# Reordering and cutting the last K and V loads of a streaming low-rank attention decode kernel

## The chip, the cores and the metric

The kernel runs on one core of a Trainium2 chip. The metric is device time in microseconds (us) of one execution, as the median of several. The profiles are single executions taken by the hardware profiler. Their span leaves out about 2 us that the device time includes (for the profiled execution of the kernel before: 258.22 us with a span of 256.2). All readings of "when" are in us from the start of the span. Program lines appear as L278 and so on. They differ between kernels, because lines were added. In the views PE is TensorE, PEld its weight loads, DVE VectorE, ACT ScalarE and SPq SyncE. The granted clock is the share of TensorE's full clock that the chip allowed (0.947 on average in the profile of the kernel before).

## The reference, cut to what matters

```python
B, H, Sq, Skv, Dh, R = 1, 32, 1, 4096, 192, 64
kp = einsum("rn,bhnd->bhrd", e_proj, k)      # project 4096 keys to 64 rows
vp = einsum("rn,bhnd->bhrd", f_proj, v)
scores = einsum("bhqd,bhrd->bhqr", q, kp) * Dh ** -0.5
p = softmax(scores)                          # over the 64 rows
o = einsum("bhqr,bhrd->bhqd", p, vp)         # one query per head
```

All tensors are bf16. K and V are 50 MB each and are read once. Everything else is small.

## The kernel before

The 32 heads are worked as 16 pairs, `m` = 0 to 15. `EP` and `FP` are `e_proj` and `f_proj` in on-chip memory, transposed; they are loaded first, as `EF`. The token index is split as 128 partitions times `J` = 32 rows, so one load brings a whole head: 128 partitions with 12,288 contiguous bytes each, 1.5 MB. Three buffers for K and three for V (`NPB`) let the loads run far ahead (35.9 us from issue to landing in the median of the K loads). In the cut below some waits for buffers are left out.

```python
# SyncE issues all loads, K pair then V pair
for m in range(NPAIR):
    slot = m % NPB
    if m >= NPB: sp.wait_ge(sem_kp, m - NPB + 1)          # buffer free again
    for i in range(2):
        sp.dma_start(K_sb[slot][:, i, :, :], seq_src(k, 2*m+i)).then_inc(sem_k[slot], 16)
    if m >= NPB: sp.wait_ge(sem_vp, vdone(m - NPB))
    for i in range(2):
        semv = sem_v[slot] if m < LASTP else sem_vlast[i]   # last pair: one semaphore a head
        sp.dma_start(V_sb[slot][:, i, :, :], seq_src(v, 2*m+i)).then_inc(semv, 16)
    if m == 0:
        sp.dma_start(Qbc[:], q2.partition_broadcast(R)).then_inc(sem_q, 16)
...
# TensorE: both heads of a pair in one matmul (384 columns), summed over 32 rows
for m in range(NPAIR):
    pe.wait_ge(sem_k[slot], 32 * (m // NPB + 1))
    for j in range(J):
        pe.matmul(kp_ps[pss][:, :, :], EP[:, j, :], K_sb[slot][:, :, j, :], start=(j == 0), stop=(j == J-1))
    if m < LASTP:
        pe.wait_ge(sem_v[slot], 32 * (m // NPB + 1))
        for j in range(J):
            pe.matmul(vp_ps[pss][:, :, :], FP[:, j, :], V_sb[slot][:, :, j, :], start=(j == 0), stop=(j == J-1))
    else:                                                  # last pair: head by head
        for i in range(2):
            pe.wait_ge(sem_vlast[i], 16)
            for j in range(J):
                pe.matmul(bank[:, 0, :], FP[:, j, :], V_sb[slot][:, i, j, :], start=(j == 0), stop=(j == J-1))
    for go in trig_out.get(m, []):                         # once for each group of 8 heads
        pe_out_group(pe, go)                               # 8 matmuls p x vp into out_ps
```

After the K matmuls, VectorE forms the scores. Once for each group of 8 heads, VectorE and ScalarE compute the softmax (about 3 us in a chain: 248.08 to 250.90 for the last group in the profile). ScalarE copies each V projection to SBUF (`VP`), and at the very end the sum to `O_sb`, which SyncE stores.

## Time and profile before

| | before |
|---|---|
| time, first four runs | 258.09 us median (258.04 to 258.35) |
| span of the profile | 256.2 us |
| one pair of loads (two DMAs) | 7.38 us |
| 32 matmuls over two heads, clock 1.0 | 5.4 us |
| last landing (last completion write of the last load) | 249.6 us |
| from there to the end | 6.6 us |

The first lines are from the profile's page of the kernel before. The rows of digits cut the span into 40 slices: the digit is the busy tenth of the 16 DMA engines, and below it is what they moved. The last line is the chain of work that ended last, by engine.

```profile
span 256.2 us, 2558 instructions
...
DMA  7999999999999999999999999999999999999970
GB/s 162 385 426 319 402 428 424 424 424 421 428 428 428 430 423 422 422 426 425 426 426 428 430 423 420 426 426 428 425 424 428 428 425 422 424 426 425 428 296 4
...
DMA 81%; PE 16%; SPq 2%; issue 0%; ACT 0%
```

The DMA engines are full from the second slice on, until the loads end within the last but one. So the stream of loads is the bound, and TensorE waits for it, as the view of waits of the same kernel shows (waiter, what it waited for, total us, number of waits, longest):

```profile
PE kp_ps L278 <- DMA K_sb<-in_k_dram: 27.9, 14, 7.0
PE vp_ps L286 <- DMA V_sb<-in_v_dram: 27.0, 15, 2.1
```

What is left is the end. This is the timeline of the kernel before (start, duration, engine, line, operation, output and inputs, count, and in brackets the idle time before and what ended it):

```profile
241.98 5.39 PE L278 MATMUL kp_ps<-K_sb,EP 128*64 128x384 bf16 x32 [1.94 <-DMA K_sb<-in_k_dram]
...
247.21 5.44 PE L298 MATMUL vp_ps<-V_sb,FP 128*64 128x192 bf16 x64
...
250.33 0.57 DVE L217 CAST PTd<-PT_g 64x1 bf16<-64x1 f32 x8
252.69 0.32 ACT L186 ACTIVATE VP<-vp_ps 64x192 bf16<-64x192 f32 x1 [2.31 <-PE vp_ps L298]
...
253.16 0.82 PE L252 MATMUL TX<-VP,PTd 64*32 64x192 bf16 x8 [0.50 <-ACT VP L186]
254.01 0.32 ACT L188 ACTIVATE O_sb<-TX 32x192 bf16<-32x192 f32 x1 [1.00 <-PE TX L252]
254.35 0.36 SPq L156 DMA_DIRECT2D out_dram<-O_sb  x1
```

The last K pair lands at 241.94. TensorE works on it until 247.2, and only then on the last V pair, although the first of its heads has landed at 245.6 by the trace's landing records: 64 matmuls of one head each, until 252.66. Then comes a fixed train: copy, eight matmuls, copy, store.

### The profile page before, as it was taken

To read this page: it belongs to the slowest core of one execution; us is meant where nothing else is said; L and a number is where in the kernel's file an instruction comes from. 1 tells how busy PE (TensorE), PEld (TensorE's weight loads), DVE (VectorE), ACT (ScalarE), POOL (GpSimd) and SP (SyncE) were. 2 spreads that over 40 slices of the span, in tenths; PEclk is the share of its full clock that TensorE was granted. 3 is DMA by queue.
4 is the path that set the end of the run, shared out by engine and by line. 5 is a ranking of instruction groups with operands and counts; after the bars stand their busy time and mean duration, and the time that the engine had idled before them with its cause. 6 is when DMAs were issued, how large, how long until landed. Compare 5 with 4: busy or idle time off the path is not lost.

```text
span 256.2 us, 2558 instructions
## 1 busy us (share of the span) xinstructions
PE 190.4 (74%) x1120; PEld 122.5 (48%) x1120; DVE 21.9 (9%) x137; ACT 13.6 (5%) x35; POOL 1.9 (1%) x14
## 2 busy tenths in 40 slices
PE   0559449668879666887966678897766799697695
PEld 0535226445546444554644445564444455364485
DVE  0400000000010020000020011000020002000021
ACT  2400000000000010000000010000000001000001
POOL 2000000000000000000000000000000000000000
PEclk9979959999979999997999999799999979799999
DMA  7999999999999999999999999999999999999970
GB/s 162 385 426 319 402 428 424 424 424 421 428 428 428 430 423 422 422 426 425 426 426 428 430 423 420 426 426 428 425 424 428 428 425 422 424 426 425 428 296 4
DMA packets 9514, 102.67 MB, mean 401 GB/s; under 512 B 1120, under 2 KB 1120, under 8 KB 1120
## 3 DMA queue, kind: packets, MB, share of 16 engines
q1 hardware_dynamic: 9504, 102.51, 96.6%
q8 instruction: 9, 0.15, 0.2%
q14 instruction: 1, 0.01, 0.0%
HBM read 102.50 MB, written 0.01 MB: 400 GB/s over the span
## 4 chain that ended last, share of the span: by engine, by line
DMA 81%; PE 16%; SPq 2%; issue 0%; ACT 0%
DMA K_sb<-in_k_dram 81%; PE kp_ps L278 13%; PE vp_ps L298 2%; SPq L147 2%; PE TX L252 0%; SPq L141 0%; SPq L140 0%; ACT VP L186 0%; ACT O_sb L188 0%
## 5 line engine op out<-in xcount | busy, mean ns | idle before, releaser
L278 PE MATMUL kp_ps<-K_sb,EP 128*64 128x384 bf16 x512 | 89.5, 335 | 27.9 <-DMA K_sb<-in_k_dram 27.9
L286 PE MATMUL vp_ps<-V_sb,FP 128*64 128x384 bf16 x480 | 88.9, 348 | 27.0 <-DMA V_sb<-in_v_dram 27.0
L278 PEld LDWEIGHTS kp_ps<-K_sb,EP 128*64 128x64 bf16 x512 | 56.4, 113 | 60.2 <-DMA K_sb<-in_k_dram 29.2
L286 PEld LDWEIGHTS vp_ps<-V_sb,FP 128*64 128x64 bf16 x480 | 54.9, 117 | 60.9 <-issue 30.7
L236 DVE CUSTOM_DVE_ANT_0 scr<-kp_ps,Qbc 64x192 bf16<-64x192 f32 x32 | 10.0, 347 | 193.5 <-PE kp_ps L278 179.6
L177 ACT ACTIVATE VP<-vp_ps 64x384 bf16<-64x384 f32 x15 | 7.3, 484 | 219.7 <-PE vp_ps L286 219.7
L266 PE MATMUL TX<-ident,EF_sb 128*128 128x128 bf16 x32 | 3.8, 310 | 8.2 <-DMA EF_sb<-in_f_proj_dram 8.2
L266 PEld LDWEIGHTS TX<-ident,EF_sb 128*128 128x128 bf16 x32 | 3.3, 164 | 8.4 <-DMA EF_sb<-in_f_proj_dram 8.2
L298 PE MATMUL vp_ps<-V_sb,FP 128*64 128x192 bf16 x64 | 5.4, 246 | 0.0
L298 PEld LDWEIGHTS vp_ps<-V_sb,FP 128*64 128x64 bf16 x64 | 5.3, 110 | 0.1
L252 PE MATMUL TX<-VP,PTd 64*32 64x192 bf16 x32 | 3.3, 243 | 0.5 <-ACT VP L186 0.5
L252 PEld LDWEIGHTS TX<-VP,PTd 64*32 64x32 bf16 x32 | 2.4, 92 | 1.6 <-issue 1.6
L208 DVE RECIPROCAL rsum<-ssum 8x1 f32<-8x1 f32 x4 | 0.6, 151 | 25.1 <-ACT Pm_g L161 25.1
L236 DVE DVE_READ_ACCUMULATOR2_ANT S_g<- 64x1 f32 x32 | 2.4, 75 | 0.0
L217 DVE CAST PTd<-PT_g 64x1 bf16<-64x1 f32 x32 | 2.3, 139 | 0.1
L227 DVE CAST EP<-TX 128x256 bf16<-128x256 f32 x4 | 1.7, 425 | 6.9 <-PE TX L266 6.8
L171 ACT ACTIVATE EP<-TX 128x256 bf16<-128x256 f32 x4 | 1.5, 385 | 8.0 <-PE TX L266 7.9
L161 ACT ACTIVATE Pm_g<-ST_g,negmx 8x64 f32<-8x64 f32 x4 | 1.3, 336 | 8.4 <-DVE negmx L204 8.4
L228 DVE CAST FP<-TX 128x256 bf16<-128x256 f32 x4 | 1.7, 414 | 0.0
L213 DVE STREAM_TRANSPOSE PT_g<-Pm_g 32x32 f32<-32x32 f32 x8 | 1.6, 200 | 0.2
L200 DVE STREAM_TRANSPOSE ST_g<-S_g 32x32 f32<-32x32 f32 x8 | 1.6, 199 | 0.2
L172 ACT ACTIVATE FP<-TX 128x256 bf16<-128x256 f32 x4 | 1.5, 377 | 0.0
(16 smaller groups left out, 8.2 us busy)
## 6 DMA issues: line engine op xcount, KB each, us to landing
K_sb<-in_k_dram SPq DMA_DIRECT2D x32, 1536.0 KB, 35.9
V_sb<-in_v_dram SPq DMA_DIRECT2D x32, 1536.0 KB, 36.5
Qbc<-in_q_dram SPq DMA_DIRECT2D x1, 768.0 KB, 22.4
EF_sb<-in_e_proj_dram SPq DMA_DIRECT2D x1, 512.0 KB, 4.9
EF_sb<-in_f_proj_dram SPq DMA_DIRECT2D x1, 512.0 KB, 6.8
out_dram<-O_sb SPq DMA_DIRECT2D x1, 12.0 KB, 1.4
```

The source lines that it names most:

```text
L147: sp.dma_start(K_sb[slot][:, i, :, :], seq_src(k, 2 * m + i)).then_inc(sem_k[slot], 16)
L177: act.activation(VP_sb[:, 2 * m:2 * m + 2, :], vp_ps[pss][:, :, :], ACT.Copy).then_inc(sem_vps_free, 1)
L200: ins = dve.transpose(ST_g[g][:, rb * TB:(rb + 1) * TB], S_g[g][rb * TB:(rb + 1) * TB, :])
L217: ins = dve.tensor_copy(PTd[:, h, h:h + 1], PT_g[g][:, i:i + 1])
L227: dve.tensor_copy(EP[:, j0:j1, :], TX[r % 2][:, 0:HJ, 0:R])
L228: dve.tensor_copy(FP[:, j0:j1, :], TX[r % 2][:, 0:HJ, R:2 * R]).then_inc(sem_evD, 1)
L236: ins = dve.tensor_tensor_reduce(out=scr[2 * pss + i][:], in0=kp_ps[pss][:, i, :], in1=Qbc[:, h, :], scale=1.0, scalar=0.0, op0=ALU.mult, ...
L252: ins = pe.matmul(out_ps, PTd[:, h, :], VP_sb[:, h, :], start=(h == 0), stop=(h == H - 1))
L266: ins = pe.matmul(TX[r % 2][:, jj, :], EF_sb[:, j::J], ident[:], start=True, stop=True)
L278: ins = pe.matmul(kp_ps[pss][:, :, :], EP[:, j, :], K_sb[slot][:, :, j, :], start=(j == 0), stop=(j == J - 1))
L286: ins = pe.matmul(vp_ps[pss][:, :, :], FP[:, j, :], V_sb[slot][:, :, j, :], start=(j == 0), stop=(j == J - 1))
L298: ins = pe.matmul(bank[:, 0, :], FP[:, j, :], V_sb[slot][:, i, j, :], start=(j == 0), stop=(j == J - 1))
```

## The change

The intent is to have less work left when the last byte lands. The change

- moves the load of the last K pair (15) ahead of the load of V pair 14;
- cuts K 15 in two, V 14 in three and V 15 in five pieces of rows, each with its own semaphore, so that TensorE can follow the stream piece by piece;
- does V 15 with matmuls over both heads again (32 instead of 64);
- does six of the last eight out matmuls after the first piece of V 15.

```diff
+    CK = [16, 16]              # rows of the pieces of K 15
+    CA = [16, 8, 8]            # V 14
+    CB = [8, 8, 8, 4, 4]       # V 15
...
+            for m in range(NPAIR - 2, NPAIR):              # SyncE: K 14 whole, then K 15 in pieces
...
+                    for c, (j0, j1) in enumerate(cuts(CK)):
+                        for i in range(2):
+                            sp.dma_start(K_sb[slot][:, i, j0:j1, :],
+                                         seq_src(k, 2 * m + i)[:, j0:j1, :]).then_inc(sem_kb[c], 16)
+            for m, sems, cs in ((NPAIR - 2, sem_va, CA), (NPAIR - 1, sem_vb, CB)):
+                sp.wait_ge(sem_vp, vdone(m - NPB))
+                for c, (j0, j1) in enumerate(cuts(cs)):
+                    for i in range(2):
+                        sp.dma_start(V_sb[slot][:, i, j0:j1, :],
+                                     seq_src(v, 2 * m + i)[:, j0:j1, :]).then_inc(sems[c], 16)
...
+            def pe_vp(m, sems, cs):                        # TensorE
+                for c, (j0, j1) in enumerate(cuts(cs)):
+                    pe.wait_ge(sems[c], 32)
+                    for j in range(j0, j1):
                         ins = pe.matmul(vp_ps[pss][:, :, :], FP[:, j, :], V_sb[slot][:, :, j, :],
                                         start=(j == 0), stop=(j == J - 1))
+                    if m == mB and c == 0:
+                        pe.wait_ge(sem_epi_p, NG)
+                        pe.wait_ge(sem_vps_free, vdone(mA))
+                        pe_out_rows(G * (NG - 1), 2 * mB)  # heads 24 to 29
+                ins.then_inc(sem_vp, 1)
+            pe_kp(mA)
+            pe_kp(mB)
+            pe_vp(mA, sem_va, CA)
+            pe_vp(mB, sem_vb, CB)
+            pe.wait_ge(sem_vps_free, vdone(mB))
+            pe_out_rows(2 * mB, H, last=True).then_inc(sem_fin, 1)
```

The first three groups of out matmuls stay where they were (after pairs 5, 9 and 13). The bytes and the arithmetic are the same.

More of the change, by code (lines that the diff above doesn't have):

```diff
@@ L43, in bass_standalone__low_rank_proj_linformer__decode_kernel @@
     AX = mybir.AxisListType
+    CK = [16, 16]
+    CA = [16, 8, 8]
+    CB = [8, 8, 8, 4, 4]
+    cuts = lambda cs: [(sum(cs[:i]), sum(cs[:i + 1])) for i in range(len(cs))]
+    assert sum(CK) == J and sum(CA) == J and sum(CB) == J
     NPB = 3
@@ L92, in bass_standalone__low_rank_proj_linformer__decode_kernel @@
         sem_v = [sem(f"sem_v{i}") for i in range(NPB)]
-        sem_vlast = [sem(f"sem_vlast{i}") for i in range(2)]
+        sem_va = [sem(f"sem_va{c}") for c in range(len(CA))]
+        sem_kb = [sem(f"sem_kb{c}") for c in range(len(CK))]
+        sem_vb = [sem(f"sem_vb{c}") for c in range(len(CB))]
         sem_kp = sem("sem_kp")
@@ L112, in bass_standalone__low_rank_proj_linformer__decode_kernel @@
         LASTP = NPAIR - 1
-        vdone = lambda m: m + 1 if m < LASTP else NPAIR + 1
+        vdone = lambda m: m + 1
         def trigger_map(lag):
@@ L122, in bass_standalone__low_rank_proj_linformer__decode_kernel @@
         trig_b = trigger_map(LAG_B)
-        trig_out = trigger_map(LAG_P)
+        trig_out = {5: [0], 9: [1], 13: [2]}
         @block.gpsimd
@@ L141, in _ @@
             sp.dma_start(EF_sb[R:2 * R, :], f_proj).then_inc(sem_ef, 16)
-            for m in range(NPAIR):
+            for m in range(NPAIR - 2):
                 slot = m % NPB
@@ L150, in _ @@
                 for i in range(2):
-                    semv = sem_v[slot] if m < LASTP else sem_vlast[i]
-                    sp.dma_start(V_sb[slot][:, i, :, :], seq_src(v, 2 * m + i)).then_inc(semv, 16)
+                    sp.dma_start(V_sb[slot][:, i, :, :], seq_src(v, 2 * m + i)).then_inc(sem_v[slot], 16)
                 if m == 0:
                     sp.dma_start(Qbc[:], q2.partition_broadcast(R)).then_inc(sem_q, 16)
+            for m in range(NPAIR - 2, NPAIR):
+                slot = m % NPB
+                sp.wait_ge(sem_kp, m - NPB + 1)
+                if m == NPAIR - 2:
+                    for i in range(2):
+                        sp.dma_start(K_sb[slot][:, i, :, :], seq_src(k, 2 * m + i)).then_inc(sem_k[slot], 16)
+                else:
+                    for c, (j0, j1) in enumerate(cuts(CK)):
[3 more added lines that the diff above has]
+            for m, sems, cs in ((NPAIR - 2, sem_va, CA), (NPAIR - 1, sem_vb, CB)):
+                slot = m % NPB
+                sp.wait_ge(sem_vp, vdone(m - NPB))
+                for c, (j0, j1) in enumerate(cuts(cs)):
+                    for i in range(2):
+                        sp.dma_start(V_sb[slot][:, i, j0:j1, :],
+                                     seq_src(v, 2 * m + i)[:, j0:j1, :]).then_inc(sems[c], 16)
             sp.wait_ge(sem_osb, 1)
@@ L174, in _ @@
                 pss = m % NPS
-                if m < LASTP:
-                    act.wait_ge(sem_vp, m + 1)
-                    act.activation(VP_sb[:, 2 * m:2 * m + 2, :], vp_ps[pss][:, :, :], ACT.Copy).then_inc(sem_vps_free, 1)
+                if m == NPAIR - 2:
+                    act_exp(act, NG - 1)
+                act.wait_ge(sem_vp, m + 1)
+                act.activation(VP_sb[:, 2 * m:2 * m + 2, :], vp_ps[pss][:, :, :], ACT.Copy).then_inc(sem_vps_free, 1)
+                if m < NPAIR - 2:
                     for g in trig_b.get(m, []):
                         act_exp(act, g)
-                else:
-                    for g in trig_b.get(m, []):
-                        act_exp(act, g)
-                    for i in range(2):
-                        act.wait_ge(sem_vp, m + 1 + i)
-                        bank = vp_ps[(pss + i) % NPS]
-                        act.activation(VP_sb[:, 2 * m + i, :], bank[:, 0, :], ACT.Copy).then_inc(sem_vps_free, 1)
             act.wait_ge(sem_fin, 1)
@@ L247, in pe_out_group @@
         def pe_out_group(pe, g):
+            assert g < NG - 1
             pe.wait_ge(sem_epi_p, g + 1)
@@ L251, in pe_out_group @@
                 h = G * g + i
-                ins = pe.matmul(out_ps, PTd[:, h, :], VP_sb[:, h, :], start=(h == 0), stop=(h == H - 1))
-            if g == NG - 1:
-                ins.then_inc(sem_fin, 1)
+                pe.matmul(out_ps, PTd[:, h, :], VP_sb[:, h, :], start=(h == 0), stop=False)
         @block.tensor
@@ L267, in _, with pe_kp @@
                 ins.then_inc(sem_tr, 1)
-            for m in range(NPAIR):
+            def pe_kp(m):
                 slot = m % NPB
                 pss = m % NPS
-                if m == 0:
-                    pe.wait_ge(sem_evD, NR)
-                    pe.wait_ge(sem_evA, NR)
-                pe.wait_ge(sem_k[slot], 32 * (m // NPB + 1))
+                if m < NPAIR - 1:
+                    pe.wait_ge(sem_k[slot], 32 * (m // NPB + 1))
                 if m >= NPS:
@@ L277, in _ @@
                 for j in range(J):
+                    if m == NPAIR - 1:
+                        for c, (j0, j1) in enumerate(cuts(CK)):
+                            if j == j0:
+                                pe.wait_ge(sem_kb[c], 32)
                     ins = pe.matmul(kp_ps[pss][:, :, :], EP[:, j, :], K_sb[slot][:, :, j, :],
@@ L280, in _, with pe_out_rows @@
                 ins.then_inc(sem_kp, 1)
+            def pe_out_rows(h0, h1, last=False):
+                for h in range(h0, h1):
+                    ins = pe.matmul(out_ps, PTd[:, h, :], VP_sb[:, h, :], start=(h == 0), stop=(last and h == h1 - 1))
+                return ins
+            pe.wait_ge(sem_evD, NR)
+            pe.wait_ge(sem_evA, NR)
+            for m in range(NPAIR - 2):
+                slot = m % NPB
+                pss = m % NPS
+                pe_kp(m)
                 if m >= NPS:
@@ L282, in _ @@
                     pe.wait_ge(sem_vps_free, m - NPS + 1)
-                if m < LASTP:
-                    pe.wait_ge(sem_v[slot], 32 * (m // NPB + 1))
-                    for j in range(J):
+                pe.wait_ge(sem_v[slot], 32 * (m // NPB + 1))
+                for j in range(J):
+                    ins = pe.matmul(vp_ps[pss][:, :, :], FP[:, j, :], V_sb[slot][:, :, j, :],
+                                    start=(j == 0), stop=(j == J - 1))
+                ins.then_inc(sem_vp, 1)
@@ L286, in _ @@
+                for go in trig_out.get(m, []):
+                    pe_out_group(pe, go)
+            mA, mB = NPAIR - 2, NPAIR - 1
+            def pe_vp(m, sems, cs):
+                slot = m % NPB
+                pss = m % NPS
+                pe.wait_ge(sem_vps_free, vdone(m - NPS))
+                for c, (j0, j1) in enumerate(cuts(cs)):
+                    pe.wait_ge(sems[c], 32)
+                    for j in range(j0, j1):
                         ins = pe.matmul(vp_ps[pss][:, :, :], FP[:, j, :], V_sb[slot][:, :, j, :],
@@ L287, in _ @@
                                         start=(j == 0), stop=(j == J - 1))
-                    ins.then_inc(sem_vp, 1)
-                else:
-                    if m >= NPB:
-                        pe.wait_ge(sem_v[slot], 32 * (m // NPB))
-                    for i in range(2):
-                        pe.wait_ge(sem_vlast[i], 16)
-                        if i == 1:
-                            pe.wait_ge(sem_vps_free, vdone(m - 1))
-                        bank = vp_ps[(pss + i) % NPS]
-                        for j in range(J):
-                            ins = pe.matmul(bank[:, 0, :], FP[:, j, :], V_sb[slot][:, i, j, :],
-                                            start=(j == 0), stop=(j == J - 1))
-                        ins.then_inc(sem_vp, 1)
@@ L301, in _ @@
-                for go in trig_out.get(m, []):
-                    pe_out_group(pe, go)
+                    if m == mB and c == 0:
+                        pe.wait_ge(sem_epi_p, NG)
+                        pe.wait_ge(sem_vps_free, vdone(mA))
+                        pe_out_rows(G * (NG - 1), 2 * mB)
+                ins.then_inc(sem_vp, 1)
+            pe_kp(mA)
[3 more added lines that the diff above has]
+            pe.wait_ge(sem_vps_free, vdone(mB))
```

## The prediction

> **What bounds the kernel.** The stream of loads. The page's 40 slices show the 16 DMA engines full from the second slice to the last but one at 420 to 430 GB/s; the chain of waits is 81% DMA. TensorE waits about 2 us for nearly every load of a head pair (two DMAs of 1.5 MB, 7.38 us for both). So only two things can change the time: the length of the stream, and what follows its last byte.
>
> **The tail before (timeline, last 30 us).** The last K pair is seen at 241.94; one V pair later, at 241.94 + 7.38 = 249.3 us (estimate), the last load has landed. But TensorE started the last K pair's 5.4 us at 241.98 and only then the 64 V matmuls of one head each, 247.2 to 252.66 (82 ns apart). Then: copy 0.33, eight out matmuls with their wait 0.97, and 2.2 from the last copy's start to the end. So 6.9 us pass after the last landing, 3.4 of them TensorE's backlog.
>
> **What the change does.**
> - It loads the last K pair ahead of the last but one V pair: the last K matmuls, scores and softmax run under the stream, about 234.7 to 243.5.
> - It cuts the last V pairs into chunks, each with its semaphore, and uses matmuls over both heads (168 ns apart, 32 instead of 64). TensorE can follow: 8 steps take 1.35 us while their chunk takes 1.84 to land; the last chunk's four take 0.67.
> - It moves six of the last eight out matmuls ahead of the last chunks.
> - It splits loads: per DMA engine 112 more packets and 14 more completion writes. In the trace's DMA records a 12,288-byte packet takes 460 ns and an 8,192-byte one 309 at best, so about 7 ns don't depend on size; a completion write takes 9. Estimate: 112 x 7 + 14 x 9 = 0.9 us of longer stream. [...]before has no packets of 1.5 to 6 KB to check it with. SyncE issues far ahead, so I expect no gap.
>
> **The new tail.** Last landing about 250.2; TensorE done 0.8 later; one copy 0.5; signal and two out matmuls 0.4; then 2.2 as before. That is 3.9 us after the last landing instead of 6.9. Net: 3.0 less in the tail, 0.9 more in the stream: 2.1 us of 258.09.
>
> **Prediction: 256.0 us, 255.1 to 257.2 in 8 of 10.** Faster by over 2%: 2%; within 2%: 97%; slower by over 2%: 1%. A saving of 2% would take 5.2 us, and 2.2 of the 6.9 are untouched.
>
> **What would show it.** In the timeline the last K matmuls end near 240, V chunks have short waits for DMA between them, under 1 us of TensorE follows the last wait for DMA, and the end comes 3.9 us after the last landing. The DMA slices stay at 420 to 430 GB/s to the last; the last landing moves by under 1.5 us. The chain is DMA nearly to its end.
>
> **What would make it wrong.** Small packets much slower than 7 ns each (tail pieces at half rate would eat about 2 us); or free packets (0.9 us more gained); SyncE held back so that a gap opens; TensorE's clock at 0.5 in the last window, as in some 3.4 us stretches before, where 32 matmuls took 7.04 instead of 5.36 us: up to 1 us of backlog [...].

## The result, and the profile after

The changed kernel takes 256.03 us (median of 10 runs, 255.72 to 256.39), beside 258.30 us for the kernel before (median of 15 runs that include those on the same chip). The ratio is 0.9911, with a 95% interval of 0.9897 to 0.9924. Ratios here are the mean time of one kernel's runs over that of the other's runs of the same rounds, so they are not quite the ratio of the medians quoted. Executions over 1.5% slower than the fastest of the same kernel are left out of the means. The gain is 2.3 us; it was predicted as 2.1.

The page of the changed kernel:

```profile
span 254.6 us, 2506 instructions
...
DMA  7999999999999999999999999999999999999991
GB/s 160 387 427 319 381 425 429 429 421 429 421 429 427 421 429 422 423 429 429 421 425 427 427 423 425 425 429 427 420 427 429 429 425 419 425 417 415 404 396 64
...
DMA 66%; SPq 19%; PE 13%; issue 1%; ACT 0%
```

And its timeline at the end:

```profile
227.58 10.59 PE L298 MATMUL kp_ps<-K_sb,EP 128*64 128x384 bf16 x64 [1.17 <-DMA K_sb<-in_k_dram]
...
238.99 5.36 PE L331 MATMUL vp_ps<-V_sb,FP 128*64 128x384 bf16 x32 [0.82 <-DMA V_sb<-in_v_dram]
...
241.12 0.57 DVE L236 CAST PTd<-PT_g 64x1 bf16<-64x1 f32 x8
...
244.86 1.46 PE L331 MATMUL vp_ps<-V_sb,FP 128*64 128x384 bf16 x8 [0.50 <-DMA V_sb<-in_v_dram]
...
248.71 2.79 PE L331 MATMUL vp_ps<-V_sb,FP 128*64 128x384 bf16 x16 [0.38 <-DMA V_sb<-in_v_dram]
250.66 0.47 PEld L331 LDWEIGHTS vp_ps<-V_sb,FP 128*64 128x64 bf16 x4 [0.18 <-DMA V_sb<-in_v_dram]
251.54 0.48 ACT L202 ACTIVATE VP<-vp_ps 64x384 bf16<-64x384 f32 x1 [6.66 <-PE vp_ps L331]
...
252.45 0.32 ACT L207 ACTIVATE O_sb<-TX 32x192 bf16<-32x192 f32 x1 [0.42 <-PE TX L304]
252.79 0.36 SPq L180 DMA_DIRECT2D out_dram<-O_sb  x1
```

The K matmuls of both last pairs now run in one piece to 238.2. The last group's softmax is done at 241.7, nine us before the last landing. TensorE waits for pieces of V (0.82, 0.50, 0.38 us) and the last piece finds it 0.85 us from done (its weights start at 250.66, the last matmul ends at 251.51). Then comes one copy, two matmuls, one copy and the store.

The trace's DMA records have 16 completion writes of 4 bytes, 9 ns each, for every load (1088 for the 68 DMAs of the kernel before). I take them as one from each of the 16 DMA engines, after its share of the load. With the last completion of the final store put at the end of the span, the last landing and the rest are as follows. (On this scale they are about 0.25 us later than the timeline shows the waiting matmuls start.)

| us | before | after | difference | predicted |
|---|---|---|---|---|
| last landing | 249.60 | 250.93 | +1.33 | +0.9 |
| from there to the end of the span | 6.56 | 3.68 | -2.88 | -3.0 |
| span | 256.16 | 254.61 | -1.55 | -2.1 |
| time, median | 258.30 | 256.03 | -2.27 | -2.1 |

The span differs by less than the time, mostly because the profiled execution of the changed kernel was one of its two slowest: its ten spans run from 253.9 to 254.6. Another 0.3 us lies outside the span (258.22 - 256.16 = 2.06 us before, 256.39 - 254.61 = 1.78 after).

Two readings of the new profile would mislead. The slices of the last loads show 417, 415, 404 and 396 GB/s where before had 426, 425, 428 and then 296, in the slice in which its loads end. Here are busy times, granted clock, DMA share and GB/s of some stretches of the changed kernel, with the last two columns the ones to read:

```profile
230.00:234.00 4.00, 4.00 (x27) 2.69 (x25) 0.64 (x4) 0.00 (x0) 0.00 (x0) 1.00 1.01 411
...
238.00:240.00 2.00, 1.18 (x9) 0.72 (x8) 1.38 (x8) 0.26 (x2) 0.00 (x0) 1.00 1.03 402
...
242.00:244.00 2.00, 2.00 (x14) 1.33 (x13) 0.00 (x0) 0.00 (x0) 0.00 (x0) 1.00 1.03 399
...
246.00:248.00 2.00, 2.00 (x15) 1.23 (x14) 0.00 (x0) 0.00 (x0) 0.00 (x0) 1.00 1.03 388
```

The engines are as busy as ever (the share is 1.01 to 1.03). They move fewer bytes in that time, because the pieces become smaller (the run with more small packets, below, shows the same in the middle of its stream: 399 to 402 GB/s instead of 425). And the chain that ended last shows SyncE with 19%, as if issuing had become a limit. The longest pieces of issuing in that chain take 1.6 to 9.2 us, the others 0.33 to 0.59. I read this as SyncE held back while enough loads are in flight, which no run tested; the DMA share shows that nothing runs dry.

### The profile page after: what moved, and what is told of

Its sections match the earlier page's. It is cut to its first block, busy times and chain, and to the rows that moved or that the text cites. A ratio compares the mean times of both kernels' runs of the same rounds, so it can differ in the third digit from the quotient of the medians.

```text
span 254.6 us, 2506 instructions
## 1 busy us (share of the span) xinstructions
PE 195.5 (77%) x1088; PEld 122.6 (48%) x1088; DVE 21.9 (9%) x137; ACT 13.4 (5%) x34; POOL 1.9 (1%) x14
## 4 chain that ended last, share of the span: by engine, by line
DMA 66%; SPq 19%; PE 13%; issue 1%; ACT 0%
DMA V_sb<-in_v_dram 36%; DMA K_sb<-in_k_dram 30%; SPq L177 11%; PE kp_ps L298 6%; PE vp_ps L317 6%; SPq L158 4%; SPq L170 1%; SPq L154 1%; PE vp_ps L331 1%; PE TX L272 0%; SPq L148 0%; SPq L147 0%; ACT VP L202 0%; SPq L160 0%; PE TX L304 0%
## 5 line engine op out<-in xcount | busy, mean ns | idle before, releaser
L298 PE MATMUL kp_ps<-K_sb,EP 128*64 128x384 bf16 x512 | 90.9, 339 | 22.0 <-DMA K_sb<-in_k_dram 22.0
L317 PE MATMUL vp_ps<-V_sb,FP 128*64 128x384 bf16 x448 | 86.8, 359 | 24.6 <-DMA V_sb<-in_v_dram 24.6
L298 PEld LDWEIGHTS kp_ps<-K_sb,EP 128*64 128x64 bf16 x512 | 57.2, 114 | 55.0 <-DMA K_sb<-in_k_dram 23.0
L331 PE MATMUL vp_ps<-V_sb,FP 128*64 128x384 bf16 x64 | 11.1, 326 | 1.7 <-DMA V_sb<-in_v_dram 1.7
L272 PE MATMUL TX<-VP,PTd 64*32 64x192 bf16 x24 | 2.5, 244 | 0.0
L272 PEld LDWEIGHTS TX<-VP,PTd 64*32 64x32 bf16 x24 | 1.8, 92 | 0.9 <-issue 0.9
```

The source lines that it names most:

```text
L272: pe.matmul(out_ps, PTd[:, h, :], VP_sb[:, h, :], start=(h == 0), stop=False)
L298: ins = pe.matmul(kp_ps[pss][:, :, :], EP[:, j, :], K_sb[slot][:, :, j, :], start=(j == 0), stop=(j == J - 1))
L317: ins = pe.matmul(vp_ps[pss][:, :, :], FP[:, j, :], V_sb[slot][:, :, j, :], start=(j == 0), stop=(j == J - 1))
L331: ins = pe.matmul(vp_ps[pss][:, :, :], FP[:, j, :], V_sb[slot][:, :, j, :], start=(j == 0), stop=(j == J - 1))
```

## The experiments

Twelve runs were made, in three sets of four; one is a repeat for its profile. The kernel before had a median of 258.37, 258.38 and 258.56 us beside them. The sets did not all run on the same chip, so across sets only differences of over 0.5 us are read. All gave correct results. The rows stand in the order of the sets.

| run | time, median | ratio to before | span |
|---|---|---|---|
| changed kernel again | 256.07 | 0.9906 | 254.5 |
| new order, nothing cut | 260.09 | 1.0067 | 258.0 |
| old order, all pieces | 256.09 | 0.9903 | 254.8 |
| old order, only V 15 cut | 258.57 | 1.0000 | 256.8 |
| changed, V 15 in two pieces | 258.54 | 0.9996 | 256.1 |
| changed, V 14 whole | 259.96 (five executions) | 1.0054 | 258.0 (second run) |
| changed, more small packets | 261.57 | 1.0113 | 260.2 |
| changed, cut by head | 256.88 | 0.9932 | 255.0 |
| changed, fetch moved | 258.76 | 0.9993 | 256.7 |
| changed, q by matmul | 249.63 | 0.9637 | 247.8 |
| same, f_proj on a second queue | 249.49 | 0.9631 | 247.8 |

Theory P, that of the prediction, is pacing: the gain is that TensorE owes few matmuls when the last byte lands, against a slightly longer stream. Theory O, its rival, is order: what pays is that the last K pair, its scores and its softmax leave the tail. The change does both.

### The changed kernel again

> The changed kernel again, as the yardstick of this chip: about 2.2 us faster than before; profiled span near 254.6, last landing to end 3.9 us.

It took 256.07 us, 2.3 us less than before on that chip. Its last landing was at 250.81, and 3.67 us followed.

### The new order without cuts

```diff
-    CK = [16, 16]
-    CA = [16, 8, 8]
-    CB = [8, 8, 8, 4, 4]
+    CK = [32]
+    CA = [32]
+    CB = [32]
```

> The new order of the loads (last K pair ahead of the last but one V pair) without any cutting. Theory P (pacing: what counts is how few matmuls TensorE still owes when the last byte lands): the last but one V pair lands whole near 242, its 32 matmuls run to 247.7, the last V pair lands near 249.5 and its 32 take 5.4 more, so span 258 to 259, 2 to 3 us SLOWER than before and over 4 slower than the changed kernel. Theory O (order: the gain is that the last scores and softmax leave the tail): most of the gain stays, 1 to 2 us faster than before.

It was 1.7 us slower than before, a little less than the 2 to 3 expected, and 4.0 slower than the changed kernel. Its TensorE timeline:

```profile
242.14 5.36 PE L331 MATMUL vp_ps<-V_sb,FP 128*64 128x384 bf16 x32 [2.03 <-DMA V_sb<-in_v_dram]
249.50 5.36 PE L331 MATMUL vp_ps<-V_sb,FP 128*64 128x384 bf16 x32 [2.00 <-DMA V_sb<-in_v_dram]
254.79 0.98 PE L304 MATMUL TX<-VP,PTd 64*32 64x192 bf16 x8
```

TensorE idles for 2 us before each whole pair, the last one too. Then all 32 matmuls of the last pair follow the landing (249.50 to 254.8), and the last eight out matmuls after them. The softmax of the last group was long done. So the new order alone gives no gain, and Theory O falls. This version differs from the kernel before in one more thing: it takes the last V pair whole and not head by head. The 2.00 us of waiting at 249.50 suggest that this, and not the order, makes it the slower one; that was not run.

### The old order with the same number of pieces

```diff
-    CK = [16, 16]
-    CA = [16, 8, 8]
+    CK = [16, 8, 8]            # K 15 now comes after V 14 again
+    CA = [16, 16]
...
-                    if m == mB and c == 0:
+                    if m == mB and c == 1:
...
             pe_kp(mA)
-            pe_kp(mB)
             pe_vp(mA, sem_va, CA)
+            pe_kp(mB)
             pe_vp(mB, sem_vb, CB)
```

(SyncE's loads and ScalarE's exp follow the same order.)

> The order of the loads as before (V of pair 14, then K of pair 15), with as many pieces as the change: V 14 in two, K 15 in 16+8+8 rows, V 15 as changed; the six early out matmuls go one piece later. Theory P: the same as the changed kernel within 0.4 us, as the softmax (3.5 us after the last K matmul, near 244.3) is done by 247.8, still before the last landing near 250.7. Theory O: the gain is lost, time within 0.7 us of before.

It took 256.09 us, the same as the changed kernel's 256.07 in the same rounds. The timeline of its end:

```profile
239.11 5.36 PE L297 MATMUL kp_ps<-K_sb,EP 128*64 128x384 bf16 x32 [0.81 <-DMA K_sb<-in_k_dram]
...
247.43 0.57 DVE L235 CAST PTd<-PT_g 64x1 bf16<-64x1 f32 x8
...
248.27 0.67 PE L303 MATMUL TX<-VP,PTd 64*32 64x192 bf16 x6
...
248.87 2.79 PE L330 MATMUL vp_ps<-V_sb,FP 128*64 128x384 bf16 x16
```

The last K matmuls end only at 244.5, and the softmax at 248.0 (the last CAST, 247.43 + 0.57). That is still in time for the six out matmuls at 248.27. So the order that the change introduces is neither sufficient (run before) nor needed (this run). The pieces are what pays. (The six early out matmuls are in every one of these versions; what they give by themselves was not run.)

### The old order, only the last load cut

```diff
-    CK = [16, 8, 8]            # against the run above
-    CA = [16, 16]
+    CK = [32]
+    CA = [32]
...
-                    if m == mB and c == 1:
+                    if m == mB and c == 2:
```

> Order as before, only the last V pair cut in five, K 15 and V 14 whole. Theory P: K 15 lands whole near 242.3, TensorE runs from there to the end without a wait (32 K and 32 V matmuls and six out matmuls, to about 253.7), span near 256.8: 0 to 1 us slower than before. Theory that cutting the last load alone gives the gain: 2 us faster than before.

It took 258.57 us, the same as before. Its TensorE timeline:

```profile
242.13 5.36 PE L297 MATMUL kp_ps<-K_sb,EP 128*64 128x384 bf16 x32 [2.04 <-DMA K_sb<-in_k_dram]
247.32 4.06 PE L330 MATMUL vp_ps<-V_sb,FP 128*64 128x384 bf16 x24
...
251.91 1.49 PE L330 MATMUL vp_ps<-V_sb,FP 128*64 128x384 bf16 x8
```

From 242.13 TensorE never waits for a load again. Its backlog comes from the 5.4 us that it owes for the K pair that landed whole, and cutting the last load doesn't reduce that. TensorE needs 5.4 us for what takes 7.38 to land, so it catches up only 2 us per pair. To be level at the end, it must already have been fed in pieces one or two loads earlier.

### V 14 whole, and V 15 in two pieces

```diff
-    CA = [16, 8, 8]            # first kernel
+    CA = [32]
-    CB = [8, 8, 8, 4, 4]       # second kernel
+    CB = [16, 16]
```

> The changed kernel with the last but one V pair whole instead of 16+8+8. Theory P: the stream is 0.3 us shorter, but TensorE, idle from 238.3 to 242.5, starts its 32 matmuls only then and never waits again: span near 257.0, 2.4 us slower than the changed kernel, though no piece of the LAST load was touched. If only the last load's cut mattered: the same as the changed kernel.

> The changed kernel with the last V pair in two pieces of 16 rows instead of five. Theory P with the prediction's sizes: 48 packets and 6 completion writes fewer per DMA engine make the stream 0.45 us shorter, but 16 steps (2.7 us) instead of 4 (0.7) follow the last landing: net 1.5 us slower than the changed kernel, span near 256.15, about 257.6 unprofiled. If small packets cost more than 8 ns, less slow.

With V 14 whole the time was 259.96 us (median of five executions), 3.9 slower than the changed kernel, where pacing gave 2.4. The profiled execution of this set was disturbed and is left out: it took 484.59 us, with K matmuls of 687 ns on average where the changed kernel has 339, so that the loads waited for TensorE. (With it the median is 260.15, hence the 4.1 us in the next expectation.) So the kernel ran once more for a profile.

> The same kernel as the run with the last but one V pair whole, for a profile in the fast state. That run was 4.1 us slower than the changed kernel where pacing alone gave 2.4. If TensorE's clock made the difference: a stretch of 3.4 us at clock 0.5 right after the 4.2 us of idle time before 242.5, the 32 V matmuls take near 7.0 us instead of 5.4, span near 258.5. If not: clock 1.0 throughout the tail and span near 257.

That run took 259.82 us. Its stretches (busy times, then granted clock, DMA share and GB/s), and its TensorE timeline:

```profile
238.00:242.00 4.00, 0.00 (x0) 0.00 (x0) 2.48 (x20) 0.44 (x2) 0.00 (x0) 0.98 0.98 404
242.00:246.00 4.00, 3.88 (x15) 2.27 (x16) 0.00 (x0) 0.00 (x0) 0.00 (x0) 0.59 1.03 400
246.00:250.00 4.00, 4.00 (x26) 2.69 (x25) 0.00 (x0) 0.48 (x1) 0.00 (x0) 1.00 0.68 249
```

```profile
242.12 8.21 PE L331 MATMUL vp_ps<-V_sb,FP 128*64 128x384 bf16 x40 [4.42 <-DMA V_sb<-in_v_dram]
...
250.85 4.09 PE L331 MATMUL vp_ps<-V_sb,FP 128*64 128x384 bf16 x24
```

The clock of the first matmuls was 0.59 on average over 242 to 246, with one stretch of 3.4 us at 0.5 from 241.9 in the trace's clock records. The first 40 matmuls took 8.21 us; at 168 ns each they take 6.7. So in this execution 1.5 us of the loss is the clock and the rest is the pacing. Four of the slow stretches of the kernel before, at 73.17, 117.55, 161.92 and 206.29, are each 44.37 us apart, 13 times their own length of 3.41 us. The stretch here follows 4.42 us of idle TensorE. Those four follow only 2.1 us of idle time each, as at the first of them in the kernel before:

```profile
72.34 7.04 PE L286 MATMUL vp_ps<-V_sb,FP 128*64 128x384 bf16 x32 [2.08 <-DMA V_sb<-in_v_dram]
```

But five other V pairs between 80 and 200 us of that profile follow as much idle time and run at full clock: the first of them, at 87.10, follows 2.09 us and takes 5.36. What sets off a slow stretch is not shown by these runs.

With V 15 in two pieces three runs took 257.72 to 257.92, which is what pacing and shorter stream gave (257.6), and three 259.16 to 259.33. The profiled one belongs to the first three and has clock 1.0 until its loads and V matmuls are done. TensorE is idle for 2.3 us before the last V pair there:

```profile
246.25 2.76 PE L331 MATMUL vp_ps<-V_sb,FP 128*64 128x384 bf16 x16 [2.31 <-DMA V_sb<-in_v_dram]
```

So the clock may be the cause of the other three. Their mean granted clocks (0.932, 0.946, 0.932, against 0.953, 0.951 and 0.945 of the faster three) lean that way, but they were not profiled, and this stays open.

### More small packets in the middle of the stream

```diff
+    CX = [8, 8, 8, 8]
+    MX = range(4, 10)          # pairs 4 to 9, K and V
...
                 for i in range(2):
-                    sp.dma_start(K_sb[slot][:, i, :, :], seq_src(k, 2 * m + i)).then_inc(sem_k[slot], 16)
+                    for j0, j1 in cuts(CX if m in MX else [J]):
+                        sp.dma_start(K_sb[slot][:, i, j0:j1, :],
+                                     seq_src(k, 2 * m + i)[:, j0:j1, :]).then_inc(sem_k[slot], 16)
```

(V alike; TensorE still waits for whole pairs, with the count raised.)

> The changed kernel with every K and V load of pairs 4 to 9 cut in four (3,072-byte packets, 72 more DMAs): 576 more packets and 72 more completion writes per DMA engine, in a stretch where no piece is waited for by itself. Cost per packet as predicted (7 to 8.3 ns, and 9 ns per completion write): the stream and the time grow by 4.7 to 5.4 us. If the extra 1.3 us of the changed kernel's stream came from something else and packets are free: no change. If SyncE's issues (0.4 us each) hold the stream back: more than 8 us, with gaps in the DMA slices.

It took 261.57 us, 5.5 more than the changed kernel, and its last landing came at 256.47 instead of 250.81: 5.66 us later. Its page:

```profile
DMA  6999999999999999999999999999999999999991
GB/s 167 389 423 302 411 429 425 423 427 420 414 401 402 402 399 400 402 401 401 400 401 402 402 399 402 426 431 425 424 429 425 423 423 424 425 420 414 404 394 54
```

The engines stay full, and the cut stretch shows 399 to 402 GB/s instead of 425. With 9 ns for each of the 72 completion writes, 5.01 us are left for 576 packets: 8.7 ns each. The records of single packets say the same. In the changed kernel the shortest 12,288-byte packet takes 460 ns, the 6,144-byte one 234, the 3,072-byte one 121 and the 1,536-byte one 65: halving a packet always leaves 8 to 9 ns over. For the change itself this makes 112 x 8.7 + 14 x 9 = 1.10 us of its 1.2 to 1.33 us of longer stream. The rest of 0.1 to 0.2 us is within what two executions of one kernel differ by.

### Cut by head instead of by rows

The same pacing needs fewer packets if the two heads of a pair are loaded one after the other: the first head then has its own landing without being cut.

```diff
-    CK = [16, 16]
-    CA = [16, 8, 8]
-    CB = [8, 8, 8, 4, 4]
+    CK = [[32], [32]]          # pieces of head 0, of head 1
+    CA = [[32], [16, 16]]
+    CB = [[16, 16], [16, 8, 8]]
```

(The matmuls of these three loads are over one head: 96 more of them.)

> A trial of a better version: the same pacing with fewer packets, by cutting the last three loads by head and piece (K 15: two whole heads; V 14: one whole head, one in two; V 15: heads in 16+16 and 16+8+8 rows), matmuls over one head there. 80 packets and 10 completion writes fewer per DMA engine: last landing 0.75 us earlier, the same 0.9 us of TensorE after it (8 steps of 82 ns). 0.6 to 0.8 us faster than the changed kernel; no faster if the packet cost is not what stretched the stream.

It was 0.8 us slower than the changed kernel (256.88; all six executions, 256.71 to 257.30, lie above that kernel's highest, 256.42), so the expectation failed. The end of its timeline:

```profile
247.09 1.51 PE L332 MATMUL vp_ps<-V_sb,FP 128*64 128x192 bf16 x16 [1.71 <-DMA V_sb<-in_v_dram]
...
249.12 2.83 PE L332 MATMUL vp_ps<-V_sb,FP 128*64 128x192 bf16 x32
```

TensorE waits 1.7 us before 247.09, more than anywhere in the changed kernel's end, and then works without a break to 251.95. A piece landed late, and the last 16 completion writes of the stream say how, one line per kernel. (Sorted by time, from the trace's DMA records; one from each of the 16 DMA engines for its share of each load, as taken above, so an engine that is late can have several among them.)

```
changed kernel   249.93 249.98 249.98 250.04 250.24 250.25 250.30 250.31 250.42 250.42 250.48 250.53 250.74 250.74 250.80 250.81
cut by head      248.67 248.72 248.74 248.74 248.75 248.87 249.20 249.44 249.44 249.63 249.68 249.69 249.70 249.71 250.16 251.11
```

All but two are at or before 249.71, 1.1 us earlier than the changed kernel's last: the saved packets did shorten the stream. But one write is 1.4 us later than that. In these records 16,384-byte packets of the queue named instruction appear about every 30 us: eight in the changed kernel, the last at 231.7, and nine in this one, the last at 245.1. I call them fetches of instructions; one takes 1.02 to 1.15 us in the first profiles of the kernel before and of the changed one. The by-head version has 96 more matmuls on TensorE, each with its weight load (1184 of each on its page, 1088 on that of the changed kernel). After each fetch in the middle of the stream, one more of the 16 engines completes its loads 1.2 to 1.5 us later than its neighbours (in the kernel before, the load after the first fetch, at 28.98, has fifteen completions at 30.12 to 30.42 and one at 31.92), and stays so while the loads are whole (among the small pieces at the changed kernel's end, first and last completion of a load move from 1.9 to under 1 us apart). In the kernel before, the whole set of completions of one load lies within 0.3 us before the first fetch; near the end it is split in two groups 1.5 us apart, and the later group decides (its last is 249.6). In the by-head version the last fetch strikes an engine that is already late. Up to the load before it, the last of the 16 completions comes 1.78 us after the first; from the next load on, 3.18 us. That next load is the one that TensorE waits for: 15 engines have landed it at 245.65, the last at 247.05 (landing records, on the timeline's scale), and the wait ends at 247.09.

### Moving the fetch

To test this, fifty small dummy matmuls were put at the start, where TensorE has nothing to do. They are meant to shift only the place in the program at which the blocks of instructions are fetched. (The first fetch moved from 29.4 to 19.9 us, so these are TensorE's.)

```diff
             pe.wait_ge(sem_ident, 1)
+            for _ in range(50):
+                pe.matmul(TX[1][:, 0, 0:64], ident[:], ident[:, 0:64], start=True, stop=True)
+            pe.wait_ge(sem_ef, 32)
```

> The changed kernel with 50 small dummy matmuls on TensorE before the transposes, while it has nothing to do. They move nothing but the places at which TensorE's instructions are fetched: a ninth fetch of 16 KB should then fall inside the last loads, near 245 to 248 us, as it did in the by-head version (245.1). Theory F (each such fetch sets one DMA engine back by about 1.4 us, and the last landing waits for that engine): last landing near 252.2 instead of 250.8, 1.0 to 1.5 us slower than the changed kernel. Rival (the fetch is harmless, the by-head version lost by its smaller DMAs or matmuls): same as the changed kernel within 0.3 us.

It took 258.76 us, 0.2 more than the kernel before in its rounds, where the changed kernel had been 2.3 less: 2.5 us are lost, 2.2 of them seen in the span (256.7 against 254.5). Its four executions took 258.48 to 259.30; the changed kernel's highest was 256.42. The ninth fetch came at 249.89, somewhat later than expected. The timeline:

```profile
249.27 1.49 PE L333 MATMUL vp_ps<-V_sb,FP 128*64 128x384 bf16 x8 [0.33 <-DMA V_sb<-in_v_dram]
...
251.73 1.82 PE L333 MATMUL vp_ps<-V_sb,FP 128*64 128x384 bf16 x8 [0.97 <-DMA V_sb<-in_v_dram]
252.70 0.46 PEld L333 LDWEIGHTS vp_ps<-V_sb,FP 128*64 128x64 bf16 x4 [0.52 <-DMA V_sb<-in_v_dram]
```

Now TensorE waits 0.97 us and then 0.5 more for the last two pieces. The last completions are

```
fetch moved      249.85 249.86 249.88 250.27 250.29 250.30 250.31 250.34 250.35 250.36 250.38 250.84 251.14 251.99 252.49 252.98
```

Twelve of them are as before. The four latest run on to 252.98, 2.2 us after the changed kernel's 250.81, with steps of 0.5 us between the last three, as one engine makes that still has the last pieces to do. The packet records bear this out: after 250.84 only one engine still moves data. By the times it is the one that carries the fetch, one packet of 1.09 us from 249.89, and then the 25 packets of 1,536 bytes that it still owes, the first five at 0.13 to 0.18 us each instead of 0.065. So here a fetch of instructions in the last us went with a last landing 2.2 us later, and delayed the kernel.

The size needs two parts. At the usual pace of 0.0615 us each, the 25 packets would have ended near 251.4, so the ninth fetch itself costs about 1.5 us, close to the 1.4 expected. The other 0.6 us that engine was late already. The dummy matmuls moved every fetch, and from the earlier first one on, one engine ends its loads 2.9 us after the first engine, where the changed kernel has 1.6; that this is the same engine fits the times, but the records do not name the engines. So this run is not a test of the ninth fetch alone. For the by-head version the records above show the late engine, but it wasn't run without its ninth fetch.

### A shorter stream

The records of the kernel before also show that loading q is dear. The q row (12 KB) is broadcast to 64 partitions, 768 KB, and the landings on either side of it are 7.5 us apart instead of 3.69. The next version loads it once to one partition and spreads it with 16 matmuls by a row of ones.

```diff
-                    sp.dma_start(Qbc[:], q2.partition_broadcast(R)).then_inc(sem_q, 16)
+            sp.dma_start(Qrow[:], q2.rearrange("(o h) d -> o h d", o=1)).then_inc(sem_q, 16)   # before K 0
...
+                for s in range(2):
+                    h = 4 * (r - NR) + 2 * s
+                    ins = pe.matmul(qps(r, s), ones[:], Qrow[:, h:h + 2, :], start=True, stop=True)
+                ins.then_inc(sem_tr, 1)        # VectorE and ScalarE copy the banks to Qbc
```

> A version to beat both: the changed kernel with q loaded once as 12 KB on one partition and spread to 64 partitions by 16 matmuls with a row of ones, in place of the 768 KB broadcast load. In the trace of before the landings either side of that load are 7.5 us apart instead of 3.69 for one load: it takes 3.8 us of the stream. If the stream's length is what counts: 3.4 to 3.9 us faster than the changed kernel, near 252.4.

> The same and f_proj issued from ScalarE's queue beside e_proj from SyncE's. In the trace of before these two loads of 512 KB on 64 partitions each take 4.95 us, one after the other (8,192-byte packets at 576 ns instead of 309). If the two halves of the partitions can then be written at once: up to 2.4 us faster than the q version alone; if they still go at half rate: no change.

The q version takes 249.63 us, ratio 0.9637 to before: 6.4 us less than the changed kernel instead of the 3.4 to 3.9 expected. Its page and the end of its timeline:

```profile
span 247.8 us, 2563 instructions
...
GB/s 163 388 431 430 427 427 436 425 434 419 436 427 431 431 427 432 427 429 425 434 423 436 421 436 427 432 433 423 434 423 434 419 436 425 438 410 426 415 410 71
```

```profile
241.74 2.94 PE L358 MATMUL vp_ps<-V_sb,FP 128*64 128x384 bf16 x16 [0.22 <-DMA V_sb<-in_v_dram]
...
244.72 0.48 ACT L215 ACTIVATE VP<-vp_ps 64x384 bf16<-64x384 f32 x1 [6.47 <-PE vp_ps L358]
```

The dip of the fourth and fifth slices (319 and 381 GB/s in the changed kernel) is gone, which is 4.2 us: the loads of V 0 and K 1 now land 3.66 us apart where 7.9 lay between them in the changed kernel. The rest comes from all over the stream: the 12,288-byte packets between 50 and 230 us take 460.6 ns on average here and 464.6 in the changed kernel and in the kernel before. Over 60 loads of 8 packets per engine that is 1.9 us. It is not the chip: the versions with V 14 whole and with the fetch moved have 464.6 and 464.7 on the same one. Why it is so is open. The end is paced as before; the new fetch at 244.08 falls with the last landing (244.09) and does no harm.

Putting f_proj on ScalarE's queue beside e_proj on SyncE's gave nothing more: 249.49 us, 0.14 less, where doubling the rate of these two loads would have brought 2.4 (an estimate: half of the 4.95 us that both take in the trace of the kernel before, with 8,192-byte packets at 576 ns on average and 309 at the shortest). Why these two loads and the broadcast of q are slow is not shown.

## Why the prediction was right, point by point

- **Bound and tail.** Right. The stream ends at 249.6, or 249.3 on the timeline's scale (predicted 249.3 from one wait and the pace of the pairs), and 6.56 us followed, predicted 6.9.
- **The new tail.** Right: 3.68 us after the last landing instead of 6.56, a saving of 2.88, predicted 3.0. The last wait of TensorE is followed by 0.85 us, predicted 0.8. By the timelines, TensorE's backlog after the last landing makes 2.5 us of the saving, and the six out matmuls moved ahead make 0.5 (0.82 to 0.34 us); the longer last copy takes 0.15 back.
- **The longer stream.** Right in kind, a little small: +1.2 to 1.33 us, predicted 0.9. A packet costs 8.7 ns and not 7. The 7 came from two sizes only (3 x 309 - 2 x 460), where 1 ns in the smaller makes 3 ns in the result.
- **The sum.** Its closeness (2.27 us against 2.1) is partly luck. In the two profiles the terms give +1.33 - 2.88 = -1.55 us. The medians come nearer because the profiled execution was a slow one and because 0.3 us was saved outside the span, where the prediction had nothing.
- **Last K matmuls near 240.** They ended at 238.2. I had overlooked in the sum that K 15 is also cut, so TensorE begins it at 233.
- **Why the reordering helps.** This was listed as the first thing that the change does, and the sum didn't need it separately. The runs show no gain from it: with pieces both orders take the same time (256.09 and 256.07), and the new order without pieces took 260.09.
- **The marks in the profile.** The last landing moved by less than 1.5 us, as said. The DMA slices did not stay at 420 to 430 GB/s to the end (417 to 396 GB/s), as my own packet cost should have told me. The chain was not DMA nearly to its end: it counts SyncE's issues, in pieces of up to 9.2 us, as work (19%).
- **Dangers named.** Small packets at half rate did not happen (388 GB/s at the least in the stretches above). The slow clock did not strike the end of the changed kernel (1.00 from 195 us on) but did strike that of the version with V 14 whole (0.59 over 242 to 246). The danger not named was the fetch of instructions. The changed kernel escapes it, and that was luck: with 32 matmuls less (1088 against 1120), it shows eight fetches and no ninth, and the ninth of the kernel before falls at 251.4, after its last load (249.6).

## What to carry to other kernels

In a kernel bound by its loads, what can be gained at the end is the work owed when the last byte lands. Compare how fast the consumer works with how fast the pieces land, and begin cutting as many loads before the last as it takes to be level; cutting only the last load, or only reordering, gained nothing here. Cut no finer than that, since every packet cost 8.7 ns per DMA engine here (with the completion writes 1.10 us, over a third of the 2.88 us that the shorter tail gained), and look first at loads in the stream that could be smaller or sent once: one broadcast load was worth more than twice the whole change.
